# The first two softmaxes ahead of the weight decode in a fused attention and MLP kernel: a reordered prologue on one core

## The chip, the core and the metric

The kernel runs on one core of one Trainium2 chip. The metric is device time in microseconds (us) of one execution, lower is better. Everything below is fp32 data; the big matmuls run as three fp32r products of a high and a low part.

## What is computed

Cut to what matters, the reference is

```python
# attention: q, k, v are (4, 8, 576, 64); factor = 4
q_d, k_d, v_d = means over groups of 4 positions            # 144 pooled positions
out_up  = repeat(softmax(q_d k_d^T / 8) v_d, 4)              # pooled attention
mask    = abs(i - j) < 4                                     # local attention
out_loc = softmax(where(mask, q k^T / 8, -1e9)) v
x = (out_up + out_loc) as (4, 576, 512)
# both softmaxes divide by (sum + 1e-9)
# MLP 1
xn = (x - mean) / sqrt(var + 1e-6) * g_ln
x  = x + relu(xn @ w_ch1) @ w_ch2                            # 512 -> 2048 -> 512
# MLP 2 (time mix with the previous position)
k = relu(xk @ w_k); v = (k * k) @ w_v; r = sigmoid(xr @ w_r)
out = r * v
```

The weights arrive as 64-bit floats and are turned into fp32 on the chip ("decoded").

## The kernel before

**Chunks and units.** The attention works on 8 chunks `c` (half a sequence, 288 positions) times 4 head pairs `hp`. One `unit(c, hp)` is the attention of a chunk for one head pair: DVE sums queries (`qd`, L251) and, in even chunks, keys (`kdz`, L255) over groups of 4; PE computes local scores (L272) and pooled scores (L276) into the PSUM tile `sc`; DVE takes the row maximum of the pooled scores (`mx<-sc`, L279), ACT the exponential (`Pd`, L283); DVE masks the local scores into `P` (L280), subtracts their maximum, ACT the exponential (L289); DVE sums (L297), adds 1e-9 (L298), inverts, scales and transposes (`T`, L304); ACT copies the transposed tile to `PT` (four copies, L308); PE transposes `Pd` (L319), multiplies by the values into `av` (L328, L335); ACT copies `ud` (L342) and DVE adds both into `x` (L343). `sc` has one buffer, so the next unit's scores wait for the exponential. `kz` (keys) holds the two heads of a pair on the two halves of the partitions, with zeros in the other half; `kdz` is laid out alike.

**MLP 1.** For every chunk, 16 feature blocks `f` go through PE: L1 (`h_ps`, 12 matmuls), a relu and split on ACT and DVE (`hh` L500, `hl` L501), L2 (`acc`, 12 matmuls). The steps of the next chunk's attention are fed in between (`slot`).

**Weight decode.** w_ch1 and w_ch2 are cut into 32 pieces of 128x512. A piece is one DMA of 512 KB (`raw`, L123), then ACT L75, DVE L76, ACT L79, DVE L80 (the fp32 value), then its split: ACT `split_hi` (L83) and DVE `split_lo` (L86). So ACT and DVE take turns, two rounds for the decode and one for the split. `conv_gen` does one piece in two steps.

**What sets the order.** The prologue is the loop before the main loop: the four units of chunk 0 and its normalisation are fed step by step, and from the 24th round on (PRO0) every second round (PRO1) takes one step of the decode. The scheduler that builds the program may move instructions of an engine against each other; those given to `in_order` keep their program order. Each engine then runs its own list strictly in that order. All loads stand in the one queue of SP; the string ORDER says in which order the first ones do (a, b: queries and keys of units 0 and 1; c: values; m: mask and vectors; w: a pair of weight pieces). After the prologue PE starts with L1 of chunk 0; the rest of the 32 pieces are decoded while PE works on chunk 0.

**MLP 2** follows after the last chunk; no line of it is changed.

Of the kernel before, what the change touches and what calls it, by code (L numbers as in the profile page):

```python
# [19 lines left out]
B, H, S, D = 4, 8, 576, 64  # L20
DM, DF, DK = 512, 2048, 1024
SD = S // 4
N = S // 2
NCH = 2 * B
NHP = H // 2
QD = SD // 2
WIN = 30
# [9 lines left out]
def tile_block(ctx: ExitStack, tc: tile.TileContext, qT, kT, vw, vr, vec, mask, w1, w2, wk, wv, wr, out):  # L37
    nc = tc.nc
# [19 lines left out]
    pin = actx.enter_context(tc.tile_pool(name="pin", bufs=2))  # L58
# [11 lines left out]
    def decode(raw, pinned=False):  # L70

        top = raw.bitcast(U8).rearrange("p (n t) -> p n t", t=8)[:, :, 3]
        rm = stg.tile([128, 2, 512], U32, tag="stg", name="rm", bufs=RB)
        ru, m = rm[:, 0], rm[:, 1]
        in_order(pinned, nc.scalar.activation(ru.bitcast(F32), raw.rearrange("p (n t) -> p n t", t=2)[:, :, 1].bitcast(F32), AF.Copy, scale=2.0 ** -112))  # L75
        in_order(pinned, nc.vector.tensor_scalar(m, ru, 0x80000000, None, op0=ALU.bitwise_and))  # L76
        yield
        low = m.bitcast(U8).rearrange("p (n t) -> p n t", t=4)[:, :, 0]
        nc.scalar.activation(low, top, AF.Copy, scale=1.0 / 32.0, bias=-31.0 / 64.0)  # L79
        nc.vector.scalar_tensor_tensor(raw[:, 0:512].bitcast(U32), ru, 3, m, op0=ALU.logical_shift_left, op1=ALU.bitwise_or)  # L80

    def split_hi(hi, w):
        nc.scalar.copy(hi, w)  # L83

    def split_lo(hi, lo, w):
        nc.vector.tensor_tensor(lo, w, hi.bitcast(F32), op=ALU.subtract)  # L86

    def wtiles(nm):
        return [wpool.tile([128, 4, 512], F32R, tag="w", name=f"{nm}{t}") for t in "hl"]
# [12 lines left out]
    def conv_gen():  # L102
        keys = list(pieces_w12())
        raws, todo = {}, iter(keys)

        def fetch():
            key = next(todo, None)
            while key in raws:
                key = next(todo, None)
            if key is None:  # L110
                return
            nm, p, k = key
            src = w1s[:, :, 1024 * p:1024 * p + 1024] if nm == "w1" else w2s[:, 4 * p:4 * p + 4, :]
            if nm == "w2" and p == 3:
                t = xp.tile([128, 1024], I32, tag=("ah", "al")[k % 2], name="raw", bufs=ABUF)
                nc.sync.dma_start(t, src[:, k])
                raws[key] = t
            else:
                t = wpool.tile([128, 2, 1024], I32, tag="w", name="raw")
                for i in range(2):  # L120
                    raws[nm, p, k + i] = t[:, i]
                for i in range(2):
                    nc.sync.dma_start(t[:, i], src[:, k + i])  # L123

        for _ in range(ORDER.count("w")):
            fetch()
            yield
        for _ in range(AHEAD - ORDER.count("w")):
            fetch()
        last = None  # L130
        for n, key in enumerate(keys + [None]):
            if last:
                split_hi(h, w)
            if key:
                nm, p, k = key
                W = W1 if nm == "w1" else W2
                if p not in W:
                    W[p] = wtiles(f"{nm}_{p}")
                raw = raws[key]
                g = decode(raw)  # L140
                next(g)
            yield
            if key:
                next(g, None)
            if last:
                split_lo(h, l, w)
                done.add(last)
            if key:
                h, l, w = W[p][0][:, k, :], W[p][1][:, k, :], raw[:, 0:512].bitcast(F32)
            last = key  # L150
            if n % 2 == 1 or n > 24:
                fetch()
            yield
# [69 lines left out]
    def load_v(c, hp):  # L223
        b, half = divmod(c, 2)
        v = pin.tile([128, 3, 2, D], F32, tag="v", name="v", bufs=3)
        nc.sync.dma_start(v, vw[b, hp, half])
        if half == 0:
            vd = pkd.tile([QD, 2, 128], F32, tag=f"vd{hp}", name="vd")
            vdt[hp] = vd
            for t in range(2):  # L230
                r = pin.tile([QD, 4, 128], F32, tag="vr", name="r", bufs=VB)
                nc.sync.dma_start(r, vr[b, hp, :, t])
                nc.gpsimd.tensor_tensor(r[:, 0:2, :], r[:, 0:2, :], r[:, 2:4, :], op=ALU.add)
                nc.gpsimd.tensor_tensor(vd[:, t, :], r[:, 0, :], r[:, 1, :], op=ALU.add)
        vts[c, hp] = v

    def unit(c, hp, nxt):
        half = c % 2
        if nxt is not None and nxt not in loaded:
            load_qk(*nxt)  # L240
        if nxt is not None and nxt not in vts:
            load_v(*nxt)
        q, k = loaded.pop((c, hp))
        v = vts.pop((c, hp))
        if hp == 0:
# [1 line left out]
        x = xt[c]  # L247
        i = hp % 2
        P, PT = Ps[i], PTs[i]
        qd = pat.tile([128, QD], F32, tag="qd", name="qd")  # L250
        nc.vector.tensor_reduce(qd, q[:, 0:N].rearrange("p (t r) -> p t r", r=4), axis=AX.X, op=ALU.add)  # L251
        if half == 0:
            for h in range(2):
                p = slice(64 * h, 64 * h + 64)
                nc.vector.tensor_reduce(kdz[hp][p, h, :], k[p, h, 3:3 + S].rearrange("p (t r) -> p t r", r=4), axis=AX.X, op=ALU.add)  # L255
        kd, vd = kdz[hp], vdt[hp]
        yield 1600 if half == 0 else 360
        if half == 0:
# [20 lines left out]
        nc.vector.tensor_reduce(m, scd, axis=AX.X, op=ALU.max)  # L279
        nc.vector.tensor_tensor(Pl.rearrange("p (h n) w -> p h n w", h=2), scl, mask_t[:, half].unsqueeze(1).to_broadcast([128, 2, 3, WIN]), op=ALU.min)  # L280
        nc.vector.tensor_scalar(m, m, -0.125 / 16.0, None, op0=ALU.mult)  # L281
        for h in range(2):
            nc.scalar.activation(Pd[:, h, :], scd[:, h, :], AF.Exp, bias=m[:, h:h + 1], scale=0.125 / 16.0, accum_out=sm[0:QD, 6 + h:7 + h])  # L283
        yield 800
# [9 lines left out]
        for h in range(2):  # L294
            nc.scalar.activation(Pd[:, h, :], Pd[:, h, :], AF.Copy, scale=mx[0:QD, 6 + h:7 + h])
        yield 400
        nc.vector.tensor_reduce(sm[:, 0:6], Pl, axis=AX.X, op=ALU.add)  # L297
        nc.vector.tensor_scalar(sm[:, 0:6], sm[:, 0:6], 1e-9, None, op0=ALU.add)  # L298
        nc.vector.reciprocal(mx[:, 0:6], sm[:, 0:6])
        yield 600  # L300
        nc.vector.tensor_tensor(Pl, Pl, mx[:, 0:6].unsqueeze(2).to_broadcast([128, 6, WIN]), op=ALU.mult)
# [264 lines left out]
    nc.scalar.copy(ones_r, ones)  # L566
    for i in range(2):
        nc.gpsimd.memset(Ps[i], 0.0)
        nc.gpsimd.memset(PTs[i], 0.0)
    for hp in range(NHP):  # L570
        nc.gpsimd.memset(kdz[hp][0:64, 1, :], 0.0)
        nc.gpsimd.memset(kdz[hp][64:128, 0, :], 0.0)
    nc.vector.tensor_scalar(omu, vec_t[:, 1:3, :], -1.0, 1.0, op0=ALU.mult, op1=ALU.add)

    first = Attn(None, 0)
    i = 0
    while not first.over():
        first.feed(PROB)
        i += 1
        if i >= PRO0 and i % PRO1 == 0:  # L580
            next(conv, None)

    def ensure(*key):
# [166 lines left out]
RB = 3  # L750
HB = 2
AHEAD = 3
PRE = 5
LB0 = 12
RATE = 900
RATEO = 1200
RATE0 = 700
PROB = 800
PRO0 = 24
PRO1 = 2  # L760
GAP = -1
ORDER = "awmbcw"
VB = 1


def _layout(inputs):
    import numpy as np

    q, k, v = (np.asarray(inputs[n]) for n in "qkv")
    f = q.dtype  # L770

    def pairsT(a, left, right):
        t = a.transpose(0, 1, 3, 2).reshape(B, NHP, 128, S)
        return np.ascontiguousarray(np.pad(t, ((0, 0), (0, 0), (0, 0), (left, right))))

    vp = np.pad(v, ((0, 0), (0, 0), (3, 5), (0, 0)))
    idx = (24 * np.arange(24)[:, None] + np.arange(32)[None, :]).reshape(2, 3, 4, 32)
    vwin = vp[:, :, idx, :].reshape(B, NHP, 2, 2, 3, 4, 32, D)
    vwin = vwin.transpose(0, 1, 3, 5, 6, 4, 2, 7).reshape(B, NHP, 2, 128, 3, 2, D)
    vr = v.reshape(B, NHP, 2, 2, QD, 4, D).transpose(0, 1, 4, 3, 5, 2, 6).reshape(B, NHP, QD, 2, 4, 128)  # L780
    vec = np.stack([np.asarray(inputs[n]).reshape(KT, 128).T for n in ("moe_g_ln", "moe2_mu_k", "moe2_mu_r")], axis=1)

    r = np.arange(32)[:, None]
    w = np.arange(WIN)[None, :]
    mask = np.empty((4, 32, 2, 3, WIN), f)
    for half in range(2):
        for n in range(3):
            for j in range(4):
                i0 = N * half + 96 * n + 24 * j
                key = i0 - 3 + w  # L790
                ok = (np.abs(i0 + r - key) < 4) & (key >= 0) & (key < S)
                mask[j, :, half, n, :] = np.where(ok, 3.0e38, -8.0e9)
    c = np.ascontiguousarray
    return {
        "qT": pairsT(q, 0, 8), "kT": pairsT(k, 3, 3), "vw": c(vwin), "vr": c(vr), "vec": c(vec),
        "mask": c(mask.reshape(128, 2, 3, WIN)),
        **{n: c(inputs[m]).view(np.int64) for n, m in WEIGHTS},
    }
# [17 lines left out]
```

## Time and profile before

| | |
|---|---|
| median of 3 runs | 803.0 us (802.44 to 803.74) |
| the profiled execution | 801.98 us, its span 799.9 us |
| busy in the span | PE 758.2 us (95%), DVE 546.4 (68%), ACT 398.7 (50%), POOL 76.6 (10%) |
| granted TensorE clock, mean | 0.998 of full speed |
| before PE's first L1 matmul (0 to 53.4 us) | PE 19.15 us busy, DVE 42.83, ACT 37.04 |

The span is the time from the first to the last instruction that the profile has. "Busy" counts an instruction from its start to its end; PE's busy share says little of how full PE is, since matmuls overlap. A line number is that of the kernel before; the changed kernel's lines are some 8 to 9 higher from `unit` on.

### The profile page before, as it was taken

The page shows a single profiled execution, that of the slowest core. Times are in us where ns is not written, and L with a number is a line of the kernel's source. Part 1 is how long each engine was busy: PE and PEld are TensorE (multiplying, and loading weights), DVE is VectorE, ACT ScalarE, POOL GpSimd, SP SyncE. Part 2 cuts the span into 40 slices and gives each one's busy share as a digit, 9 for nine tenths or more (in the row PEclk, how much of TensorE's full clock was granted, in tenths as well). Part 3 has the DMA queues.
Part 4 walks back from the last instruction along what each step waited for, and adds up shares of the span by engine and source line. Part 5 has one row for each costly group of instructions (what it writes and reads, how often), then busy time and mean ns, then how long its engine had stood idle before and what let it go on. Part 6 is the DMA issues. An engine that isn't in the chain of part 4 may idle for free.

```text
span 799.9 us, 15611 instructions
## 1 busy us (share of the span) xinstructions
PE 758.2 (95%) x6150; PEld 731.3 (91%) x6150; DVE 546.4 (68%) x1234; ACT 398.7 (50%) x995; POOL 76.6 (10%) x121
## 2 busy tenths in 40 slices
PE   2559989999999999999999999999999999999998
PEld 1349989999999999999999999999999999999998
DVE  6989997655665746665755645846959586867664
ACT  4889975543553543544553543734444353525140
POOL 3210332001131001121001001001000000000000
PEclk9999999999999999999999999999999999999999
DMA  7796533332342331451333310522020202010101
GB/s 223 231 319 230 175 100 107 114 101 79 111 142 92 105 103 58 120 163 59 109 89 109 86 50 30 186 79 70 11 69 6 74 1 80 1 40 1 41 1 40
DMA packets 43209, 76.06 MB, mean 95 GB/s; under 512 B 4608, under 2 KB 28288, under 8 KB 43136
## 3 DMA queue, kind: packets, MB, share of 16 engines
q1 hardware_dynamic: 43136, 75.07, 29.8%
q8 instruction: 48, 0.79, 0.4%
q14 instruction: 25, 0.20, 0.1%
HBM read 60.38 MB, written 14.68 MB: 94 GB/s over the span
## 4 chain that ended last, share of the span: by engine, by line
PE 83%; DVE 7%; DMA 5%; ACT 4%; issue 1%; SPq 0%; ACTq 0%
PE b_ps L196 10%; PE b_ps L195 10%; PE b_ps L197 10%; PE h_ps L195 8%; PE acc L195 7%; PE acc L196 7%; PE acc L197 7%; PE h_ps L196 7%; PE h_ps L197 7%; DMA raw<-in_w 4%; PE av L328 2%; PE sc L276 2%; PE sc L272 2%; DVE raw L80 1%; PE tp L319 1%; PE av L335 1%
## 5 line engine op out<-in xcount | busy, mean ns | idle before, releaser
L501 DVE SCALAR_TENSOR_TENSOR hl<-h_ps,hh 128x288 fp32r<-128x288 f32 x128 | 57.8, 453 | 85.5 <-ACT hh L500 85.0
L500 ACT ACTIVATE hh<-h_ps 128x288 fp32r<-128x288 f32 x128 | 51.6, 405 | 80.1 <-PE h_ps L197 79.3
L197 PE MATMUL b_ps<-xk,wbl 128*128 128x384 f32 x192 | 64.9, 338 | 0.0
L195 PE MATMUL b_ps<-xk,wbh 128*128 128x384 f32 x192 | 64.9, 338 | 0.0
L196 PE MATMUL b_ps<-xk,wbh 128*128 128x384 f32 x192 | 64.8, 338 | 0.0
L197 PE MATMUL b_ps<-k,wbl 128*128 128x384 f32 x192 | 64.1, 334 | 0.0
L195 PE MATMUL b_ps<-k,wbh 128*128 128x384 f32 x192 | 64.1, 334 | 0.0
L196 PE MATMUL b_ps<-k,wbh 128*128 128x384 f32 x192 | 64.1, 334 | 0.0
L728 DVE RECIPROCAL e<-e 128x384 f32<-128x384 f32 x24 | 61.1, 2544 | 0.1
L308 ACT COPY PT<-T 32x144 f32<-32x144 f32 x128 | 39.6, 309 | 32.5 <-DVE T L304 31.1
L521 POOL TENSOR_TENSOR x<-x2t,x 128x288 f32<-128x288 f32 x32 | 25.4, 826 | 294.7 <-DVE x2t L520 236.4
L708 ACT ACTIVATE kr<-b_ps 128x384 f32<-128x384 f32 x48 | 23.5, 490 | 46.9 <-PE b_ps L197 46.9
L647 ACT ACTIVATE mixa<-x2in,vec_t 128x384 f32<-128x384 f32 x48 | 28.1, 613 | 37.3 <-DVE xr L650 34.8
L80 DVE SCALAR_TENSOR_TENSOR raw<-rm 128x512 uint32<-128x512 uint32 x52 | 37.2, 720 | 12.0 <-ACT rm L79 11.7
L709 DVE TENSOR_TENSOR kr<-kr,b_ps 128x384 f32<-128x384 f32 x48 | 26.5, 552 | 25.8 <-ACT kr L708 25.8
L79 ACT ACTIVATE rm<-raw 128x512 uint8<-128x512 uint8 x52 | 39.9, 784 | 7.0 <-DVE rm L76 6.7
L283 ACT ACTIVATE Pd<-sc,mx 72x144 f32<-72x144 f32 x64 | 23.4, 370 | 37.6 <-DVE mx L281 37.5
L195 PE MATMUL acc<-hh,w_1h 128*128 128x288 f32 x128 | 40.4, 319 | 1.0 <-ACT hh L500 1.0
L195 PE MATMUL h_ps<-ah,w_0h 128*128 128x288 f32 x128 | 39.4, 309 | 1.2 <-ACT ah L394 1.2
L698 DVE TENSOR_TENSOR k<-kr,k 128x384 fp32r<-128x384 f32 x48 | 26.7, 556 | 19.8 <-ACT k L697 19.7
L195 PE MATMUL h_ps<-ah,w_2h 128*128 128x288 f32 x128 | 40.0, 312 | 0.0
L195 PE MATMUL acc<-hh,w_2h 128*128 128x288 f32 x128 | 39.9, 315 | 0.0
(160 smaller groups left out, 2560.4 us busy)
## 6 DMA issues: line engine op xcount, KB each, us to landing
raw<-in_w SPq DMA_DIRECT2D x32, 512.0 KB
v<-in_vw SPq DMA_DIRECT2D x32, 192.0 KB
bd<-raw SPq DMA_DIRECT2D x20, 256.0 KB
wf<-bd SPq DMA_DIRECT2D x10, 512.0 KB
q<-in_qT SPq DMA_DIRECT2D x32, 148.0 KB
kz<-in_kT SPq DMA_DIRECT2D x32, 145.5 KB
r<-in_vr SPq DMA_DIRECT2D x32, 144.0 KB
x2d<-x SPq DMA_DIRECT2D x8, 576.0 KB
```

Of the source, the lines that this page charges most:

```text
L79: nc.scalar.activation(low, top, AF.Copy, scale=1.0 / 32.0, bias=-31.0 / 64.0)
L80: nc.vector.scalar_tensor_tensor(raw[:, 0:512].bitcast(U32), ru, 3, m, op0=ALU.logical_shift_left, op1=ALU.bitwise_or)
L195: nc.tensor.matmul(ps, wh, ah, start=first, stop=False)
L196: nc.tensor.matmul(ps, wh, al, start=False, stop=False)
L197: nc.tensor.matmul(ps, wl, ah, start=False, stop=last)
L308: nc.scalar.copy(PT[p, :, j, :], T[p, :, 0:24])
L500: nc.scalar.activation(hh, ps[:, 0:N], AF.Relu)
L501: nc.vector.scalar_tensor_tensor(hl, ps[:, 0:N], 0.0, hh.bitcast(F32), op0=ALU.max, op1=ALU.subtract)
L647: nc.scalar.activation(a2, t[:, k, :, 1:SEG + 1], AF.Copy, scale=vec_t[:, 1 + which, k:k + 1])
L698: nc.vector.tensor_tensor(l, r, h.bitcast(F32), op=ALU.subtract)
L709: nc.vector.tensor_tensor(r, r, ps[:, 0:NB], op=ALU.mult)
L728: nc.vector.reciprocal(e, e)
```

## The change

Four things. The unit's sums are cut out into `prep`, which makes one instruction of the two key sums (over 128 partitions and both heads; the zeros of `kz` give the zeros of `kdz`, whose clearing on POOL goes); in chunk 0 the next unit's `prep` is called inside the unit, right behind its maximum, and keeps its program order. All steps of the first PINNED = 6 pieces keep their program order. The addition of 1e-9 to the local sums (L298) goes: column 30 of `P` is set to 1e-9 once, and the sum takes 31 columns; the host clears the two spare rows of the value windows. ORDER puts the first weight pair behind the mask and the second unit's queries and keys, and the decode takes two of every five rounds, from the 5th on.

```diff
-        nc.scalar.activation(low, top, AF.Copy, scale=1.0 / 32.0, bias=-31.0 / 64.0)
-        nc.vector.scalar_tensor_tensor(raw[:, 0:512].bitcast(U32), ru, 3, m, ...)
+        in_order(pinned, nc.scalar.activation(low, top, AF.Copy, scale=1.0 / 32.0, bias=-31.0 / 64.0))
+        in_order(pinned, nc.vector.scalar_tensor_tensor(raw[:, 0:512].bitcast(U32), ru, 3, m, ...))
...
         for n, key in enumerate(keys + [None]):
+            pin = n < PINNED
             if last:
-                split_hi(h, w)
+                in_order(pin, split_hi(h, w))
...
-                g = decode(raw)
+                g = decode(raw, pin)
...
-                split_lo(h, l, w)
+                in_order(pin, split_lo(h, l, w))
...
+    def prep(c, hp):
+        q, k = loaded[c, hp]
+        qd = pat.tile([128, QD], F32, tag="qd", name="qd")
+        qds[c, hp] = qd
+        in_order(c == 0, nc.vector.tensor_reduce(qd, q[:, 0:N].rearrange("p (t r) -> p t r", r=4), axis=AX.X, op=ALU.add))
+        if c % 2 == 0:
+            in_order(c == 0, nc.vector.tensor_reduce(kdz[hp], k[:, :, 3:3 + S].rearrange("p h (t r) -> p h t r", r=4), axis=AX.X, op=ALU.add))
...
+        if (c, hp) not in qds:
+            prep(c, hp)
...
-        qd = pat.tile([128, QD], F32, tag="qd", name="qd")
-        nc.vector.tensor_reduce(qd, q[:, 0:N]...)
-        if half == 0:
-            for h in range(2):
-                p = slice(64 * h, 64 * h + 64)
-                nc.vector.tensor_reduce(kdz[hp][p, h, :], k[p, h, 3:3 + S]...)
+        qd = qds.pop((c, hp))
...
         nc.vector.tensor_scalar(m, m, -0.125 / 16.0, None, op0=ALU.mult)
+        if c == 0 and nxt in loaded:
+            prep(*nxt)
...
-        nc.vector.tensor_reduce(sm[:, 0:6], Pl, axis=AX.X, op=ALU.add)
-        nc.vector.tensor_scalar(sm[:, 0:6], sm[:, 0:6], 1e-9, None, op0=ALU.add)
+        nc.vector.tensor_reduce(sm[:, 0:6], P[:, :, 0:WIN + 1], axis=AX.X, op=ALU.add)
...
+        nc.gpsimd.memset(Ps[i][:, :, WIN:WIN + 1], 1e-9)
-    for hp in range(NHP):
-        nc.gpsimd.memset(kdz[hp][0:64, 1, :], 0.0)
-        nc.gpsimd.memset(kdz[hp][64:128, 0, :], 0.0)
...
-        if i >= PRO0 and i % PRO1 == 0:
+        if i >= PRO0 and i % 5 in (0, 2):
             next(conv, None)
...
+PINNED = 6
-PRO0 = 24
-PRO1 = 2
+PRO0 = 5
-ORDER = "awmbcw"
+ORDER = "ambwcw"
...
+    vwin[..., WIN:, :] = 0
```

How the built programs differ, at the three places that the prediction speaks of. `kz_106` and `kz_107` are the two key buffers, `P_112`/`PT_104` those of the first (and third) unit, `P_113`/`PT_105` those of the second (and fourth).

SP's queue from its start, before:

```order
L215 DMA q<-in_qT 128x296
L220 DMA kz_106<-in_kT 64x582 x2
L123 DMA raw<-in_w 128x1024 x2
L556 DMA mask_t<-in_mask 128x180
L557 DMA vec_t<-in_vec 128x12
L215 DMA q<-in_qT 128x296
L220 DMA kz_107<-in_kT 64x582 x2
L226 DMA v<-in_vw 128x384
```

and in the changed kernel:

```order
L217 DMA q<-in_qT 128x296
L222 DMA kz_106<-in_kT 64x582 x2
L565 DMA mask_t<-in_mask 128x180
L566 DMA vec_t<-in_vec 128x12
L217 DMA q<-in_qT 128x296
L222 DMA kz_107<-in_kT 64x582 x2
L123 DMA raw<-in_w 128x1024 x2
L228 DMA v<-in_vw 128x384
```

The first weight pair moved behind five other loads. (On ACT the first decode step, L75 of the first piece, stands ahead of the first unit's exponential in both programs.)

ACT from the first unit's `PT` copies and the second unit's exponential to the first unit's `ud`, before:

```order
L308 COPY PT_104<-T 32x6x24 x4
L283 ACTIVATE Pd,sm<-sc,mx 72x144 x2
L289 ACTIVATE P_113<-P_113 128x6x30
L79 ACTIVATE rm<-raw 128x512
L342 COPY ud<-av 128x72
```

and in the changed kernel:

```order
L293 ACTIVATE Pd,sm<-sc,mx 72x144 x2
L299 ACTIVATE P_113<-P_113 128x6x30
L317 COPY PT_104<-T 32x6x24 x3
L83 CAST w_0h<-raw 128x512
L75 ACTIVATE rm<-raw 128x512
L317 COPY PT_104<-T 32x6x24
L305 ACTIVATE Pd<-Pd,mx 72x144 x2
L79 ACTIVATE rm<-raw 128x512
L317 COPY PT_105<-T 32x6x24 x4
L83 CAST w_0h<-raw 128x512
L75 ACTIVATE rm<-raw 128x512
L351 COPY ud<-av 128x72
```

Ahead of `ud` there are now two L83, two L75, the scaling of the second unit's `Pd` (two) and its four `PT` copies.

DVE from the first unit's `x` to the third unit's pooled maximum, before:

```order
L343 TENSOR_TENSOR x<-av,ud 128x288
L255 TENSOR_REDUCE kdz_110<-kz_106 64x144 x2
L298 TENSOR_SCALAR sm<-sm 128x6
L76 TENSOR_SCALAR rm<-rm 128x512
L299 RECIPROCAL mx<-sm 128x6
L301 TENSOR_TENSOR P_113<-P_113,mx 128x6x30
L279 TENSOR_REDUCE mx<-sc 72x2
```

and in the changed kernel:

```order
L352 TENSOR_TENSOR x<-av,ud 128x288
L80 SCALAR_TENSOR_TENSOR raw<-rm 128x512
L86 TENSOR_TENSOR w_0l<-raw,w_0h 128x512
L244 TENSOR_REDUCE qd<-q 128x72
L76 TENSOR_SCALAR rm<-rm 128x512
L246 TENSOR_REDUCE kdz_110<-kz_106 128x288
L80 SCALAR_TENSOR_TENSOR raw<-rm 128x512
L86 TENSOR_TENSOR w_0l<-raw,w_0h 128x512
L287 TENSOR_REDUCE mx<-sc 72x2
```

The rest of the second unit's softmax moved ahead of `x`; in its place stand the third unit's query sum and the ends of two weight pieces.

## Rows read from the trace of the kernel before

**Rows 1.** Windows: us of stretch, busy us of PE, PEld, DVE, ACT, POOL (instructions), clock, DMA.

```profile
0.00:14.30 14.30, 2.03 (x26) 0.94 (x26) 7.11 (x13) 4.45 (x6) 6.14 (x23) 1.00 0.77 226
14.30:53.40 39.10, 17.12 (x176) 11.61 (x176) 35.72 (x94) 32.59 (x85) 10.20 (x14) 1.00 0.78 248
...
80.00:100.00 20.00, 20.00 (x216) 18.75 (x216) 19.76 (x54) 19.64 (x50) 6.36 (x8) 1.00 0.58 175
...
200.00:300.00 100.00, 100.00 (x989) 95.26 (x989) 60.79 (x174) 49.23 (x146) 13.15 (x20) 1.00 0.35 111
```

**Rows 2.** Waits of PE from 53 to 160 us: total, times, longest.

```profile
PE tp L319 <- ACT Pd L295: 2.4, 1, 2.4
...
PE h_ps L196 <- DVE al L397: 0.6, 1, 0.6
```

**Rows 3.** Timeline of PE: start, duration, instruction, idle before.

```profile
53.42 0.85 PE L195 MATMUL h_ps<-ah,w_0h 128*128 128x288 f32 x2 [1.21 <-ACT ah L394]
```

**Rows 4.** Timeline of SP's queue, the issues of loads.

```profile
1.18 1.19 SPq L220 DMA_DIRECT2D kz<-in_kT  x2
2.41 1.06 SPq L123 DMA_DIRECT2D raw<-in_w  x2
3.51 0.43 SPq L556 DMA_DIRECT2D mask_t<-in_mask  x1
...
6.96 0.58 SPq L226 DMA_DIRECT2D v<-in_vw  x1
...
14.95 0.36 SPq L215 DMA_DIRECT2D q<-in_qT  x1
```

**Rows 5.** Timeline of ACT in the prologue.

```profile
7.86 0.66 ACT L75 ACTIVATE rm<-raw 128x512 f32<-128x512 f32 x1 [5.25 <-DMA raw<-in_w]
...
15.34 0.38 ACT L283 ACTIVATE Pd<-sc,mx 72x144 f32<-72x144 f32 x1 [3.19 <-DVE mx L281]
...
19.08 1.27 ACT L308 COPY PT<-T 32x144 f32<-32x144 f32 x4
...
22.27 0.72 ACT L295 ACTIVATE Pd<-Pd,mx 72x144 f32<-72x144 f32 x2
```

**Rows 6.** Timeline of DVE in the prologue.

```profile
4.29 1.53 DVE L255 TENSOR_REDUCE kdz<-kz 64x144 f32<-64x576 f32 x2 [0.84 <-DMA kz<-in_kT]
...
14.33 0.45 DVE L279 TENSOR_REDUCE mx<-sc 72x2 f32<-72x288 f32 x1
...
18.25 0.45 DVE L279 TENSOR_REDUCE mx<-sc 72x2 f32<-72x288 f32 x1
...
22.86 0.45 DVE L343 TENSOR_TENSOR x<-av,ud 128x288 f32<-128x288 f32 x1
...
26.08 0.45 DVE L279 TENSOR_REDUCE mx<-sc 72x2 f32<-72x288 f32 x1
...
34.60 0.41 DVE L279 TENSOR_REDUCE mx<-sc 72x2 f32<-72x288 f32 x1
```

**Rows 7.** Groups by line, 0 to 53.4 us: busy us, mean ns, idle before.

```profile
L75 ACT ACTIVATE rm<-raw 128x512 f32<-128x512 f32 x13 | 8.5, 659 | 5.7 <-DMA raw<-in_w 5.7
L80 DVE SCALAR_TENSOR_TENSOR raw<-rm 128x512 uint32<-128x512 uint32 x10 | 7.5, 747 | 2.3 <-ACT rm L79 2.3
...
L255 DVE TENSOR_REDUCE kdz<-kz 64x144 f32<-64x576 f32 x8 | 5.9, 744 | 1.0 <-DMA kz<-in_kT 0.8
L86 DVE TENSOR_TENSOR w_0l<-raw,w_0h 128x512 fp32r<-128x512 f32 x7 | 5.3, 753 | 0.2 <-ACT w_0h L83 0.2
...
L76 DVE TENSOR_SCALAR rm<-rm 128x512 uint32<-128x512 uint32 x12 | 4.9, 415 | 3.1 <-ACT rm L75 3.1
...
L83 ACT CAST w_0h<-raw 128x512 fp32r<-128x512 f32 x7 | 4.3, 615 | 0.0
...
L251 DVE TENSOR_REDUCE qd<-q 128x72 f32<-128x288 f32 x5 | 2.2, 435 | 0.8 <-DMA q<-in_qT 0.8
...
L298 DVE TENSOR_SCALAR sm<-sm 128x6 f32<-128x6 f32 x4 | 1.6, 406 | 0.1
```

More of the change, by code (lines that the diff above doesn't have):

```diff
@@ L78, in decode @@
         low = m.bitcast(U8).rearrange("p (n t) -> p n t", t=4)[:, :, 0]
-        nc.scalar.activation(low, top, AF.Copy, scale=1.0 / 32.0, bias=-31.0 / 64.0)
-        nc.vector.scalar_tensor_tensor(raw[:, 0:512].bitcast(U32), ru, 3, m, op0=ALU.logical_shift_left, op1=ALU.bitwise_or)
+        in_order(pinned, nc.scalar.activation(low, top, AF.Copy, scale=1.0 / 32.0, bias=-31.0 / 64.0))
+        in_order(pinned, nc.vector.scalar_tensor_tensor(raw[:, 0:512].bitcast(U32), ru, 3, m, op0=ALU.logical_shift_left, op1=ALU.bitwise_or))
     def split_hi(hi, w):
-        nc.scalar.copy(hi, w)
+        return nc.scalar.copy(hi, w)
     def split_lo(hi, lo, w):
-        nc.vector.tensor_tensor(lo, w, hi.bitcast(F32), op=ALU.subtract)
+        return nc.vector.tensor_tensor(lo, w, hi.bitcast(F32), op=ALU.subtract)
     def wtiles(nm):
@@ L200, in tile_block @@
     loaded = {}
+    qds = {}
     vdt = {}
@@ L249, in unit @@
         P, PT = Ps[i], PTs[i]
-        qd = pat.tile([128, QD], F32, tag="qd", name="qd")
-        nc.vector.tensor_reduce(qd, q[:, 0:N].rearrange("p (t r) -> p t r", r=4), axis=AX.X, op=ALU.add)
-        if half == 0:
-            for h in range(2):
-                p = slice(64 * h, 64 * h + 64)
-                nc.vector.tensor_reduce(kdz[hp][p, h, :], k[p, h, 3:3 + S].rearrange("p (t r) -> p t r", r=4), axis=AX.X, op=ALU.add)
+        qd = qds.pop((c, hp))
         kd, vd = kdz[hp], vdt[hp]
```

## The prediction, made before the changed kernel ran

> **What bounds the kernel now.** I read the table of windows first, then PE's waits, then the prologue on SP, ACT and DVE by their timelines. From the first L1 matmul at 53.42 us [rows 3] PE works without a break: in the stretch 200 to 300 it is busy all the time while DVE has 61 and ACT 49 of 100 us [rows 1]. So an instruction saved on DVE or POOL in chunks 1 to 7 is worth nothing, and only two things can move the end: when the first L1 matmul starts, and what PE waits for in chunk 0. In the prologue PE is idle most of the time; DVE is busy 35.7 of the 39.1 us from 14.3 on [rows 1], with two sorts of work that share it: four attention units and ten weight pieces. In chunk 0 DVE and ACT are full too (19.76 and 19.64 of 20 us between 80 and 100) [rows 1], and PE waits there twice, 2.4 us for the scaled `Pd` and 0.6 us for `al` [rows 2].
>
> **The sum** is made against the profiled execution (801.98 us, 1.0 under the median of 803.0); the change that it gives is added to the median.
>
> *Small edits.* L298 goes 32 times, 4 of them in the prologue (1.6 us of DVE there [rows 7]). One key sum over 1152 columns replaces two over 576 at 744 ns each [rows 7]: between 744 ns (if the halves ran at once) and 1.49 us; since both heads' columns now pass through every partition I take 1.35, two of the old less one start. The sum over 31 instead of 30 columns, the clearing of column 30 (POOL) and the clearings that go (POOL, before anything waits) I cost at nothing: POOL is busy 6 of the first 14 us [rows 1]. Were POOL's cover gone, it would be some tenths, once. In chunks 1 to 7 all this lies beside a full PE.
>
> *First exponential.* It used to come at 15.34 [rows 5], because the second unit's sums and two pieces stood ahead of the first maximum at 14.33 [rows 6]. Now the sums of unit 1 lead to a maximum at about 8.5, but on ACT the first L75 still stands ahead of the exponential, and it waits for a weight load that now stands behind five others. Those took SP from 3.51 to 6.96 [rows 4], 3.45 us, so the load is issued at 5.9, or at 5.0 if the second q load takes the 0.36 us that the third took [rows 4] in place of its 1.2; I take 5.45. Issue to L75's start was 7.86 - 2.41 = 5.45 us [rows 4, 5]; that gives 10.9. With L75 (0.66) the exponential comes at 11.6: **3.7 us earlier**. The second unit's maximum then falls on 18.25 - 3.7 = 14.55 [rows 6].
>
> *Second maximum to first `x`.* This took 22.86 - 18.25 = 4.6 us [rows 6]. ACT's list now has, ahead of `ud`, two L83 (615 ns), two L75 (659 ns) [rows 7], four `PT` copies (1.27) and two scalings of `Pd` (0.72) [rows 5] that it did not have there: 4.5 us, and ACT runs its list in order, so `ud` and DVE's `x` wait for them. `x` falls on 14.55 + 4.6 + 4.5 = 23.7. **The lead is gone**: 0.8 us later than before.
>
> *First `x` to third maximum.* Before, 26.08 - 22.86 = 3.2 us [rows 6]. Now DVE has between them `x` (0.45 [rows 6]), two L80 (747), two L86 (753), `qd` (435), L76 (415 ns) [rows 7] and the key sum (1.35): 5.65 us, less 0.5 for starts that overlap the end before by some 0.07 each, plus the turns with ACT: idle ahead of L80 and L76 is 2.3/10 and 3.1/12 us in the mean [rows 7], 0.7 for these three. Makes 5.9, so the third maximum falls on 29.6, **3.5 us late**. The third unit's scores wait for the key sum, and PE, ACT and the `PT` copies for them.
>
> *Third to fourth maximum.* Before 8.5 us [rows 6], with four decode instructions of DVE in it; the new order has eight: three more L76, one more L80, 2.0 us by their means [rows 7], 1.0 for their turns with ACT, less L298 (0.4) and 0.5 of overlapping starts. So 2.1 more: **5.6 late**, at 40.2 in place of 34.60.
>
> *Fourth maximum to L1.* Before 53.42 - 34.60 = 18.8 us [rows 3, 6] with 21 decode instructions of DVE; now 16: two L76, one L80, two L86 fewer, 3.1 us by their means less 0.3 of overlap. So 16.0: the first L1 matmul at 56.2, **2.8 us late**. In all the order up to the normalisation's first row holds eleven ends of pieces (L86) where it held ten, so the prologue does one piece more, not less.
>
> *Chunk 0.* PE's list there is unchanged, but it starts later beside the same full DVE and ACT. Followed with the same means, the new order removes the 2.4 us wait for `Pd`, keeps the 0.6, and brings three: 0.8 before the first unit of chunk 1 multiplies by its values, 0.6 at the last low halves of w_3, 2.5 at an `acc` that takes a late `hl`. 4.5 against 3.0: **+1.5**, an estimate; its bounds are -2.4 (the wait for `Pd` goes, nothing comes) and +4.
>
> Sum: +2.8 + 1.5 = +4.3 us, 806.3 for a profiled execution and **807.3 us** for the median.
>
> **A page against this sum.** The term that everything hangs on is the 5.45 us from issue to landing. The other row for it is that of the keys: issued at 1.18, their sum starts at 4.29 [rows 4, 6], 3.1 us for 146 KB. The Trainium skill, "DMA: Bandwidth & Descriptors", section "Anatomy of one DMA", fits a DMA as 2.0 us and the bytes at 436 GB/s, which makes an estimate of 3.2 us for the 512 KB of a piece; the row of the piece disagrees, that of the keys (2.3 by the fit) is nearer. What a short landing would do is the second rival.
>
> **Rivals.**
> 1. *The lead survives (faster).* If ACT and DVE kept up, DVE's work alone would set the start: 7.11 + 35.72 [rows 1], plus one piece (415 + 747 + 753 ns), less 1.6 for L298 and 0.5 for the key sums [rows 7], is 42.6 us; with the old idle of 7.2 in the head less 3.7, and 3.4 after it, L1 starts at 49.5: 3.9 us early, 799.1. It decides at the first `x`: at or before 20 us, and the third maximum at or before 23. For it: DVE is the fullest engine, and less is asked of it early. Against it: the pinned order on ACT ahead of `ud`. Chance 0.07.
> 2. *Weights land quickly.* The 5.45 us were the first loads of the program, and the keys needed only 3.1. By that the piece is there 2.35 us sooner and the whole chain with it: 805.0. That is what the page's fit makes of it. Against it: three q and k loads now stand directly ahead of the piece in the queue. Chance 0.17.
> 3. *Chunk 0 absorbs it (no change).* DVE and ACT pace chunk 0; one piece less (1.9 us of DVE) is left for it, so of 2.8 only 0.9 arrive, and with the wait for `Pd` gone -1.5: about 803. For it: both are full there. Against it: PE has no slack to catch up with, its matmuls stand back to back. Chance 0.12.
> 4. *Worse.* The load is issued at 5.9 and chunk 0's new waits come at their upper end: 2.8 + 0.4 + 4 = 7.2, 810.2. Chance 0.11.
>
> That the change doesn't do what it says is part of this: the first two maxima do move ahead of the decode, but the decode then stands ahead of units 3 and 4.
>
> **How the numbers follow.** Forecast 0.53; rivals 0.07, 0.17, 0.12, 0.11. Faster by over 0.2% (1.6 us, about what a measurement of this kernel can tell from no change) is rival 1: 0.07. Within it is rival 3: 0.12. Slower is the rest: 0.81. The range goes from 803.2, which takes in the upper half of rival 3, to 810.6, the end of rival 4; it leaves out rival 1, half of rival 3 and a tail above, some 0.18.
>
> **What would show it.** Right step by step: ACT's first L75 at 10 to 11.5 with a wait for the load ahead of it; second maximum near 14.5; first `x` near 23.7 with ACT busy ahead of `ud`; maxima of units 3 and 4 near 29.6 and 40; first L1 near 56; chunks 1 to 7 as before; PE's waits in chunk 0 some 4 us in place of 3. Wrong: a first L75 before 9; a first `x` before 22, or a third maximum before 27; a first L1 before 54; or a time lost or won after chunk 0, where I have none.

## The result, and the profile after

The changed kernel takes **808.69 us** (median of 4 runs, 807.14 to 809.11) against 802.72 us (median of 4, 801.97 to 803.74): ratio 1.0074, 95% interval 1.0059 to 1.0089, slower. The forecast was 807.3 in a range of 803.2 to 810.6. The profiled execution took 808.65 us, its span 806.9 against 799.9. One execution among all the runs of this document, one of the kernel without pins, took 1253.89 us at a mean granted clock of 0.577, a slower state, and is left out of every number here.

All but 0.2 us of the 7.0 is lost before chunk 1. PE's first L1 matmul:

```profile
59.24 0.61 PE L196 MATMUL h_ps<-ah,w_0h 128*128 128x288 f32 x1 [1.24 <-ACT ah L403]
```

It starts 5.8 us late [rows 3]. As the end of chunk 0 I take the start of the 385th matmul record of the MLP (a few records are missing, so this is good to some 0.3 us): 131.07 against 124.29, 6.8 us late. The next chunk takes 61.4 us in both.

**Where the time is.** The windows up to chunk 1, of the changed kernel (columns as in [rows 1]):

```profile
0.00:14.30 14.30, 4.54 (x56) 2.47 (x56) 7.09 (x17) 4.55 (x12) 4.04 (x16) 1.00 0.76 235
14.30:59.20 44.90, 15.26 (x146) 9.87 (x146) 35.13 (x85) 34.53 (x83) 10.33 (x16) 1.00 0.70 219
59.20:131.10 71.90, 68.78 (x595) 64.29 (x596) 65.32 (x155) 58.83 (x139) 14.78 (x17) 0.98 0.55 180
0.00:131.10 131.10, 88.58 (x797) 76.62 (x798) 107.54 (x255) 97.92 (x232) 29.14 (x48) 0.99 0.62 199
```

and of the kernel before, where [rows 1] has the first two:

```profile
53.40:124.30 70.90, 67.78 (x595) 63.75 (x596) 66.52 (x161) 60.69 (x141) 15.35 (x17) 0.98 0.57 186
0.00:124.30 124.30, 86.93 (x797) 76.30 (x798) 109.35 (x266) 97.72 (x231) 31.70 (x54) 0.99 0.66 210
```

Read the third figure, DVE. Up to chunk 1 it has 1.8 us *less* work (107.54 for 109.35), and is idle 23.6 us in place of 14.9. Of the 8.6 us more, none is in the first 14.3 us (7.2 in both), 6.4 lie between there and the first L1 matmul (44.90 - 35.13 = 9.8 against 39.10 - 35.72 = 3.4), and 2.2 in chunk 0. The change saved work on the fullest engine and paid with its idle time. What DVE waits for between 14.3 us and L1, after:

```profile
DVE raw L80 <- ACT rm L79: 3.2, 5, 1.4
DVE mx L287 <- PE sc L284: 3.2, 1, 3.2
DVE rm L76 <- ACT rm L75: 2.0, 2, 1.0
DVE w_1l L86 <- ACT w_1h L83: 0.5, 1, 0.5
```

and before:

```profile
DVE sm L292 <- ACT Pd L283: 1.3, 2, 1.0
DVE raw L80 <- ACT rm L79: 1.1, 2, 0.8
DVE w_0l L86 <- ACT w_0h L83: 0.2, 1, 0.2
```

Two new idle times: one wait of 3.2 us for the third unit's pooled scores, and 4.1 us more for ACT's steps of the decode (L80 2.1, L76 2.0).

**The one wait of 3.2 us.** All engines around it, after (the timeline, as in [rows 3]):

```profile
24.76 0.72 POOL L235 TENSOR_TENSOR r<-r 72x256 f32<-72x256 f32 x1 [5.61 <-DMA r<-in_vr]
...
26.37 0.33 SPq L234 DMA_DIRECT2D r<-in_vr  x1
...
26.84 0.83 PE L280 MATMUL sc<-kz,q 128*32 128x60 f32 x24
...
28.51 0.68 DVE L86 TENSOR_TENSOR w_0l<-raw,w_0h 128x512 fp32r<-128x512 f32 x1
...
30.18 0.45 POOL L236 TENSOR_TENSOR vd<-r 72x128 f32<-72x128 f32 x1
...
30.68 0.50 PE L344 MATMUL av<-PdT,vd 72*64 72x72 f32 x2 [3.02 <-POOL vd L236]
...
31.11 1.24 PE L284 MATMUL sc<-kdz,qd 128*72 128x288 f32 x2
...
32.38 0.45 DVE L287 TENSOR_REDUCE mx<-sc 72x2 f32<-72x288 f32 x1 [3.19 <-PE sc L284]
```

DVE is through with its decode work at 28.51 + 0.68 = 29.2. The third unit's pooled scores (L284) stand in PE's list behind the second unit's product with the pooled values (L344), which waits 3.0 us until POOL has made `vd`. In the kernel before PE's list had the scores (L276) ahead of those products (L335), and the values were there early:

```profile
18.07 0.33 SPq L232 DMA_DIRECT2D r<-in_vr  x1
...
20.80 0.72 POOL L233 TENSOR_TENSOR r<-r 72x256 f32<-72x256 f32 x1 [2.75 <-DMA r<-in_vr]
...
21.60 0.46 POOL L234 TENSOR_TENSOR vd<-r 72x128 f32<-72x128 f32 x1
...
24.81 1.23 PE L276 MATMUL sc<-kdz,qd 128*72 128x288 f32 x2
...
25.36 0.59 POOL L234 TENSOR_TENSOR vd<-r 72x128 f32<-72x128 f32 x1
...
29.24 0.45 PE L335 MATMUL av<-PdT,vd 72*64 72x72 f32 x4
```

(A wait of PE for `vd` is not new in itself: the kernel before has one of 2.99 us at 47.46, for the fourth unit. New is its place, ahead of the third unit's scores.) Why `vd` is late stands in SP's queue of the changed kernel:

```profile
16.07 0.89 SPq L123 DMA_DIRECT2D raw<-in_w  x2
19.18 0.33 SPq L234 DMA_DIRECT2D r<-in_vr  x1
19.60 0.34 SPq L217 DMA_DIRECT2D q<-in_qT  x1
20.03 1.11 SPq L222 DMA_DIRECT2D kz<-in_kT  x2
26.37 0.33 SPq L234 DMA_DIRECT2D r<-in_vr  x1
...
31.09 0.34 SPq L217 DMA_DIRECT2D q<-in_qT  x1
```

The raw values `r` have one buffer: each load waits in SP's queue until POOL has pooled the one before, and everything behind it waits too. The early decode put a weight pair (two loads of 512 KB) at 16.07 into this chain. The `r` issued at 19.18 is used by POOL at 24.76, 5.6 us later; before, the one issued at 18.07 was used at 20.80, 2.7 us later. The kernel before shows the same delay where a pair goes ahead of a value load later on: pair at 22.90, the `r` behind it issued at 25.98 and used at 30.89, 4.9 us later. In the changed kernel the loads behind that chain are late from then on: the fourth unit's queries are issued at 31.09, where they went at 18.90.

**Chunk 0.** PE's waits from 54 to 160 us, after, to set against [rows 2]:

```profile
PE acc L197 <- DVE hl L510: 2.5, 1, 2.5
PE mean L377 <- DVE xsum L364: 1.8, 1, 1.8
PE h_ps L196 <- ACT ah L403: 1.2, 1, 1.2
PE av L337 <- ACT PdT L331: 0.3, 1, 0.3
```

The second and third still belong to the prologue. The wait for `Pd` is gone, that of an `acc` for `hl` came. A shorter one shows only in PE's weight loads (PEld), for the low halves of w_3:

```profile
PEld h_ps L198 <- DVE w_3l L86: 0.8, 4, 0.3
```

### The profile page after: what moved, and what is told of

It is laid out like the page before. It is cut to its first block, busy times and chain, and to the rows that moved or that the text cites. A ratio compares the mean times of both kernels' runs of the same rounds, so it can differ in the third digit from the quotient of the medians.

```text
span 806.9 us, 15566 instructions
## 1 busy us (share of the span) xinstructions
PE 759.8 (94%) x6150; PEld 731.5 (91%) x6150; DVE 538.2 (67%) x1186; ACT 398.2 (49%) x995; POOL 73.6 (9%) x115
## 4 chain that ended last, share of the span: by engine, by line
PE 83%; DMA 5%; ACT 5%; DVE 3%; SPq 1%; issue 1%; POOL 1%; ACTq 0%; POOLq 0%; DVEq 0%
PE b_ps L197 10%; PE b_ps L196 10%; PE b_ps L198 10%; PE h_ps L196 8%; PE h_ps L197 7%; PE acc L196 7%; PE h_ps L198 7%; PE acc L197 7%; PE acc L198 7%; DMA r<-in_vr 3%; PE av L337 2%; PE sc L284 2%; DMA raw<-in_w 2%; PE sc L280 1%; ACT rm L79 1%; ACT rm L75 1%
## 5 line engine op out<-in xcount | busy, mean ns | idle before, releaser
L510 DVE SCALAR_TENSOR_TENSOR hl<-h_ps,hh 128x288 fp32r<-128x288 f32 x128 | 57.8, 453 | 90.8 <-ACT hh L509 90.1
L317 ACT COPY PT<-T 32x144 f32<-32x144 f32 x128 | 39.5, 309 | 18.9 <-DVE T L313 17.4
L715 ACT ACTIVATE kr<-b_ps 128x384 f32<-128x384 f32 x48 | 23.6, 491 | 46.9 <-PE b_ps L198 46.9
L80 DVE SCALAR_TENSOR_TENSOR raw<-rm 128x512 uint32<-128x512 uint32 x52 | 36.8, 711 | 12.1 <-ACT rm L79 11.7
L293 ACT ACTIVATE Pd<-sc,mx 72x144 f32<-72x144 f32 x64 | 23.5, 369 | 41.2 <-DVE mx L289 41.2
L79 ACT ACTIVATE rm<-raw 128x512 uint8<-128x512 uint8 x52 | 40.2, 785 | 2.6 <-DVE rm L76 2.4
L197 PE MATMUL acc<-hl,w_2h 128*128 128x288 f32 x128 | 38.1, 298 | 2.5 <-DVE hl L510 2.5
L235 POOL TENSOR_TENSOR r<-r 72x256 f32<-72x256 f32 x32 | 27.5, 859 | 136.9 <-DMA r<-in_vr 136.9
```

Source lines behind the costliest of these rows:

```text
L79: in_order(pinned, nc.scalar.activation(low, top, AF.Copy, scale=1.0 / 32.0, bias=-31.0 / 64.0))
L80: in_order(pinned, nc.vector.scalar_tensor_tensor(raw[:, 0:512].bitcast(U32), ru, 3, m, op0=ALU.logical_shift_left, op1=ALU.bitwise_or))
L197: nc.tensor.matmul(ps, wh, al, start=False, stop=False)
L317: nc.scalar.copy(PT[p, :, j, :], T[p, :, 0:24])
L510: nc.vector.scalar_tensor_tensor(hl, ps[:, 0:N], 0.0, hh.bitcast(F32), op0=ALU.max, op1=ALU.subtract)
```

## The experiments

Each theory is about which part of the change carries the loss. The first four runs do one part alone or undo one; the next ones undo two or three, then work on the value loads. Intervals are for the ratio to the kernel before on the same chip.

**The small edits alone.** The loads, the pace and the free order of the kernel before, with the key sum in one instruction and the spare column:

```diff
-PINNED = 6
+PINNED = 0
-        if i >= PRO0 and i % 5 in (0, 2):
+        if i >= PRO0 and i % 2 == 0:
-        if c == 0 and nxt in loaded:
-            prep(*nxt)
-ORDER = "ambwcw"
+ORDER = "awmbcw"
```

(PRO0 is 24 again as well, and the sums are free in their order.)

> The spare column for eps, the single key sum and the sums cut out into prep, with the order of loads, the pace of the decode and the free order of its instructions as before. My theory (the loss comes from the pinned decode ahead of the units and from the values' loads behind the weight pairs): no difference, 802 to 804 us, first L1 matmul within 1 us of 53.4. Rival (the small edits cost by themselves, for instance the 1152-column key sum on DVE): 2 us or more above before, with the first L1 late.

Measured: 803.87 us, ratio 1.0019 (1.0009 to 1.0030). The first L1 matmul at 52.97. As expected they are not the loss, but they don't pay either, although DVE's work up to chunk 1 is 0.4 us less: by the interval they cost 0.7 to 2.4 us.

**The old order of the first loads**, all else as changed:

```diff
-ORDER = "ambwcw"
+ORDER = "awmbcw"
```

> The changed kernel with the loads in the old order (first weight pair ahead of mask and second unit). Theory: the pinned decode still stands ahead of the units, so still 4 to 7 us above before; first L1 near 57 to 59. Rival (the weight pair behind five loads is what costs, since ACT's first step waits for it): back to within 1.5 us of before.

Measured: 809.67, ratio 1.0089 (1.0076 to 1.0102), 7.3 us above before; first L1 matmul at 57.24, chunk 0 75.4 us long. The order of the first loads alone doesn't carry the loss.

**No pins**, all else as changed:

```diff
-PINNED = 6
+PINNED = 0
```

> The changed kernel with PINNED = 0: the first six pieces may be moved by the scheduler again. Theory: units 1 to 4 are no longer held up behind decode instructions, the fourth maximum comes some 2 us earlier and the first L1 1.5 to 3 us earlier than in the changed kernel; total 804 to 807. If the late pooled values of unit 2 stay (3 us wait of PE for vd near 28), the gain stops there. Rival (pins don't matter, the pace does): same as the changed kernel, 808 to 809.

Measured: 809.9, ratio 1.0081 (1.0065 to 1.0098), a miss of my 804 to 807 and near the rival's 808 to 809. The fourth maximum comes 1.9 us and the first L1 matmul 1.4 us earlier than in the changed kernel (41.88 and 57.83), but chunk 0 is 73.7 us long and gives it back. The third maximum stays at 32.43, and PE's waits from 20 to 60 us still have the late values:

```profile
PE av L344 <- POOL vd L236: 2.7, 1, 2.7
```

So the early pace alone, without pins, gives the late units 3 and 4.

**The old pace**, with pins and the new loads:

```diff
-        if i >= PRO0 and i % 5 in (0, 2):
+        if i >= PRO0 and i % 2 == 0:
-PRO0 = 5
+PRO0 = 24
```

> The changed kernel with the old pace (decode from the 24th round, every second), pins and load order as changed. Theory: the decode stands behind the units again, third and fourth maximum 3 to 8 us earlier than in the changed kernel (near 26 and 32), first L1 at 52.5 to 55; but the six pinned pieces now fall later and chunk 0 pays for it, by 3 us or more: total 805 to 811. Rival (the early pace alone is the loss and nothing else): at or below before, 801 to 803.

Measured: 809.5, ratio 1.0080 (1.0067 to 1.0094). The maxima of units 3 and 4 come at 25.3 and 32.22 and the first L1 matmul at 53.80: the prologue is as good as before. But chunk 0 takes 76.4 us, and PE's waits there (from 54 to 140 us) are now for weights:

```profile
PE acc L196 <- ACT w_2h L83: 2.2, 1, 2.2
PE acc L196 <- ACT w_3h L83: 1.2, 1, 1.2
```

DVE is busy only 30.13 of the 39.5 us from 14.3 on (windows), 5.6 less than before [rows 1]: it waits 5.5 us there for ACT's decode steps (L75 3.3, L79 2.2), and the work falls to chunk 0 (69.14 us of DVE there against 66.52). The waits are not all of the longer chunk: PE is idle 5.8 us of it against 3.1, and busy 2.8 us longer (70.62 against 67.78), with a granted clock of 0.94 in the mean against 0.98.

**Pace and pins undone together**, the new loads and the sums moved ahead kept: the two edits above in one.

> The changed kernel with two parts undone together: the old start and pace of the weight decode (from pass 24 of the first chunk's prologue, every second pass) and no pieces of it pinned in place. The new order of the first loads, the sums of query and key moved ahead and the small edits stay. Theory A (pins and pace are two faces of one thing, decode work put ahead of what the first chunk's units need: early pace delays units 3 and 4 by the late pooled values, late pace with pins makes chunk 0 some 5 us longer; either alone is enough for the loss): the first matmul of chunk 0 at 51.5 to 53, chunk 0 71 to 72.5 us long, chunk 1 at 122 to 125, time 801 to 805. Theory B (the loss is in what stays: the new order of the loads, with weights landing late, and the small edits): as slow as the changed kernel, 807 to 810, chunk 1 at 129 or later.

Measured: **802.43**, ratio 0.9995 (0.9978 to 1.0012): no difference from before. First L1 matmul at 52.53, chunk 0 70.6 us. The windows:

```profile
14.30:52.50 38.20, 15.14 (x148) 9.57 (x146) 33.25 (x81) 31.67 (x79) 10.98 (x15) 0.70 0.75 247
52.50:123.10 70.60, 67.58 (x600) 62.65 (x601) 65.50 (x156) 59.98 (x141) 14.41 (x17) 0.97 0.56 188
```

With the new loads kept, neither undone costs 6 us (808.69), either one undone some 7 (809.5, 809.9), both undone none (802.43). The two parts don't add: theory A holds, theory B falls.

**The old loads as well** (ORDER as in the second run, on top of the last).

> As the run before, and the old order of the first loads too: of the change only the sums moved ahead and the small edits are left. Theory A: 802 to 805, like the small edits alone (803.9), first matmul of chunk 0 at 52.5 to 54. Theory B: faster by 3 us or more than the run before, since the load order is undone. A third reading (moving the sums ahead is itself a cost, as VectorE serves unit 2 before unit 1's exponential): slower than the small edits alone by over 1.5 us, that is 805.5 or more.

Measured: 803.19, ratio 1.0003 (0.9994 to 1.0012); first L1 matmul at 53.14. Theory A again. The order of the loads and the sums moved ahead make no difference that can be told.

**A small dose of the early pace**: no pins, old pace, two passes brought forward:

```diff
-        if i >= PRO0 and i % 2 == 0:
+        if i in (5, 10) or i >= PRO0 and i % 2 == 0:
```

> The changed kernel with the pins gone and the old pace (the run of 802.43), but two passes of the weight decode brought forward to the prologue's passes 5 and 10: a small dose of the early pace. Theory A (a pass taken early puts its weight pair and its decode work ahead of what units 3 and 4 need, on the one SP queue and in VectorE's order): the third maximum of the pooled scores 28.5 to 31 instead of 25.95, the first matmul of chunk 0 at 53 to 54.5 instead of 52.53, time 803.5 to 806. Rival (there is room for early decode while VectorE idles in units 1 and 2; only the full early pace overfills it): third maximum 25 to 27, first matmul of chunk 0 at or before 52.7, chunk 0 no longer than 70.6, time 800.5 to 802.8.

Measured: 805.08, ratio 1.0023 (1.0012 to 1.0034); third maximum at 31.80 (0.8 later than theory A had it), first L1 matmul at 54.41. The rival is refuted. The two passes brought one weight pair into the chain of value loads, at 15.71, and that pair is enough to make the values late:

```profile
15.71 0.90 SPq L123 DMA_DIRECT2D raw<-in_w  x2
...
18.95 0.33 SPq L234 DMA_DIRECT2D r<-in_vr  x1
...
23.95 1.20 POOL L235 TENSOR_TENSOR r<-r 72x256 f32<-72x256 f32 x1 [5.03 <-DMA r<-in_vr]
```

In the run before this one with the new loads (802.43) no weight load stands between 8.7 and 23.5 us, and the same `r` goes at 18.59 and is used at 21.07. One pair costs 2.5 us of landing (5.0 against 2.5), and PE then waits 3.0 us for `vd` at 30.09, as in the changed kernel.

**Two buffers for the raw values**, in the changed kernel:

```diff
-VB = 1
+VB = 2
```

> The changed kernel with two buffers instead of one for the raw values that GpSimd pools, so that a load of them no longer waits for the pooling of the one before. Theory A (3 us of the 5.8 by which chunk 0 starts late are TensorE's wait for pooled values, at 30.7 in the changed kernel's trace): the wait of 3.0 us at 30.7 is gone, the third maximum of the pooled scores comes before 30.5 instead of 32.38, the first matmul of chunk 0 at 56 to 58.5 instead of 59.24, time 805 to 808. Theory B (VectorE and ScalarE are so filled with pinned decode work that the wait only hides it): the wait goes, the first matmul of chunk 0 stays within 1 us of 59.24, time 808 to 809.5. Theory C (the values are late because the DMA queues are full of weights, not because of the single buffer): the wait at about 30.7 stays at 2 us or more.

Measured: 809.45, ratio 1.0079 (1.0067 to 1.0092). None of the three as written: the wait for `vd` goes (against C), the third maximum hardly moves, 32.12 (against A), the first L1 matmul comes 1.6 us earlier at 57.67 (against B), and the time is B's. PE:

```profile
27.03 0.83 PE L280 MATMUL sc<-kz,q 128*32 128x60 f32 x24 [1.57 <-DMA kz<-in_kT]
30.31 1.24 PE L284 MATMUL sc<-kdz,qd 128*72 128x288 f32 x2 [2.44 <-DVE kdz L246]
```

and DVE:

```profile
28.91 1.35 DVE L246 TENSOR_REDUCE kdz<-kz 128x288 f32<-128x1152 f32 x1
30.17 1.17 DVE L80 SCALAR_TENSOR_TENSOR raw<-rm 128x512 uint32<-128x512 uint32 x1
31.26 0.94 DVE L86 TENSOR_TENSOR w_0l<-raw,w_0h 128x512 fp32r<-128x512 f32 x1
32.12 0.44 DVE L287 TENSOR_REDUCE mx<-sc 72x2 f32<-72x288 f32 x1
```

With the values in time, the keys are late (the next in the same queue behind weights), then the key sum and the pinned pieces ahead of the maximum. Three latenesses lie one under the other; taking away the top one shows the next.

**The same in the kernel before** (VB = 2, nothing else).

> The kernel before with two buffers for the raw values, nothing else: the control of the run before, and a version that could be faster than both. If the single buffer costs the kernel before too, the first matmul of chunk 0 comes at 48 to 51.5 instead of 53.42 and the time is 800 to 802.5 if chunk 0 keeps its 70.9 us; if chunk 0 then meets its weights late, chunk 0 is 73 to 79 us long and the time is 803 to 808. If the single buffer costs the kernel before nothing, within 1 us of the kernel before.

Measured: 805.93, ratio 1.0037 (1.0023 to 1.0051). The first L1 matmul does come 3.8 us earlier, at 49.63, and chunk 0 takes 80.0 us:

```profile
14.30:49.60 35.30, 17.05 (x176) 11.11 (x176) 30.06 (x82) 26.93 (x75) 9.24 (x16) 1.00 0.92 321
49.60:129.60 80.00, 73.11 (x620) 66.35 (x621) 71.50 (x170) 65.51 (x151) 12.76 (x18) 0.96 0.47 153
```

DVE did 5.7 us less between 14.3 us and L1 than before [rows 1] and 5.0 more in chunk 0 (71.50 against 66.52). An earlier L1 with less decoded is no gain. PE's waits in chunk 0 are not for weights, as I had expected (0.2 us): they are for the attention of chunk 1, 2.7 us for `Pd` and 2.1 for `PdT`. Why chunk 0 is as much as 9.1 us longer is not shown in full.

**The values through GpSimd's own queue**, in the changed kernel:

```diff
-                nc.sync.dma_start(r, vr[b, hp, :, t])
+                nc.gpsimd.dma_start(r, vr[b, hp, :, t])
```

> The changed kernel with the raw values loaded by GpSimd's own DMA queue instead of SP's, so that SP no longer stands still behind a load that waits for the pooling before it. Theory A1 (SP's standing still makes the queries and keys of units 3 and 4 late): those of unit 4 are issued before 26 instead of 31.09, the third maximum comes before 30 instead of 32.38, the first matmul of chunk 0 at 55 to 57.5 instead of 59.24; time 805 to 808.5, the less if chunk 0 then waits for weights. Theory A2 (what is late is late because weights take the transfer's time, in whatever queue; as with two buffers): the third maximum stays at 31.5 or later, the first matmul of chunk 0 at 57.5 or later, time 808 to 810.

Measured: 814.68, ratio 1.0144 (1.0129 to 1.0160), a miss for both: the third maximum comes at 27.76, as A1 had it, the first L1 matmul at 61.71, later than either. SP no longer stands still and issues 24 weight pieces by 60 us where the changed kernel issued 19, and the values land later: 6.6 us in the median, against 2.5 to 5.6 from issue to use in the changed kernel (behind the first). DMA issues from 0 to 60 us (KB each, median us to landing):

```profile
raw<-in_w SPq DMA_DIRECT2D x24, 512.0 KB, 7.8
...
r<-in_vr POOLq DMA_DIRECT2D x9, 144.0 KB, 6.6
```

PE waits for `vd` 3.4 us at 33.64 and 4.0 us at 47.24.

**The same on the version of 802.43.**

> The same edit on the kernel with pace and pins undone (802.43): a version that could be faster than both. TensorE waited 3.9 us there for the pooled values of unit 4, at 47.5. If the single chain of value loads through SP costs it time: the first matmul of chunk 0 at 48.5 to 51 instead of 52.53 and, with chunk 0 at its 70.6 us, 799 to 801. If chunk 0's end is set by the weight decode, as the kernel before with two value buffers suggests (its chunk 0 began 3.8 us earlier and took 9.1 us longer): chunk 0 is longer by as much or more, time 802 to 807.

Measured: 812.72, ratio 1.0119 (1.0105 to 1.0133), a miss too: first L1 matmul at 59.97. PE's waits up to 140 us:

```profile
PE av L344 <- POOL vd L236: 10.8, 4, 6.5
```

In both of these a separate queue gave the small loads nothing; the weights beside them had no stop any more. The Trainium skill, "DMA: Bandwidth & Descriptors", section "Issuing engines are not separate DMA queues", has the rule: all issuing engines share the same 16 DMA engines. The landing times (6.6 us against 2.5 to 5.6) agree with it; that it is the whole cause was not shown here, since the issue by GpSimd itself changed too.

**All runs together.** DVE's busy and idle time up to chunk 1, from the windows of each run's profiled execution (us); the last column is the median of its runs (the two kernels' own from the result; the experiments ran on three chips, where the kernel before has 802.41, 802.87 and 803.18). Work plus idle is the start of chunk 1 by definition; what the table adds is that the work hardly differs:

| run | first L1 | DVE work | DVE idle | chunk 1 | median |
|---|---|---|---|---|---|
| pace and pins undone | 52.5 | 106.0 | 17.1 | 123.1 | 802.43 |
| kernel before | 53.4 | 109.4 | 14.9 | 124.3 | 802.72 |
| pace, pins and loads undone | 53.1 | 105.0 | 19.6 | 124.6 | 803.19 |
| small edits alone | 53.0 | 108.9 | 16.2 | 125.1 | 803.87 |
| two early passes | 54.4 | 107.0 | 20.6 | 127.6 | 805.08 |
| before, two value buffers | 49.6 | 109.7 | 19.9 | 129.6 | 805.93 |
| old pace | 53.8 | 107.1 | 23.1 | 130.2 | 809.50 |
| **changed kernel** | 59.2 | 107.5 | 23.6 | 131.1 | 808.69 |
| no pins | 57.8 | 106.9 | 24.6 | 131.5 | 809.90 |
| two value buffers | 57.7 | 108.4 | 23.2 | 131.6 | 809.45 |
| old loads | 57.2 | 108.5 | 24.2 | 132.7 | 809.67 |
| values' own queue, pace and pins undone | 60.0 | 106.2 | 28.2 | 134.4 | 812.72 |
| values' own queue | 61.7 | 110.3 | 24.5 | 134.8 | 814.68 |

The work spans 5.3 us without following the time; the idle spans 13 and follows it in the large, though not row by row (19.6 at 803.19, 19.9 at 805.93). The first L1 matmul alone does not (49.6 and 53.8 in slow kernels).

## Why the prediction was right, and where a step failed

The time was held by the range, and the sign and mechanism (the softmaxes move ahead, the decode then stands ahead of units 3 and 4) were as forecast. That it was held with a term missing is in part luck: on the profiled executions the sum said +4.3 us and +6.7 came (808.65 against 801.98), and the range reached that far up for rival 4, whose chain did not occur. By its steps:

- *First exponential.* Predicted load issue 5.45, first L75 10.9, exponential 11.6. Measured 5.14, 10.27 and 10.84:

```profile
10.27 0.66 ACT L75 ACTIVATE rm<-raw 128x512 f32<-128x512 f32 x1 [7.65 <-DMA raw<-in_w]
10.84 0.36 ACT L293 ACTIVATE Pd<-sc,mx 72x144 f32<-72x144 f32 x1
```

  The landing took 10.27 - 5.14 = 5.13 us, near the 5.45 of [rows 4, 5]. Rival 2, weights that land quickly, is refuted. The prediction's estimate of 3.2 us for this load, from the fit in the Trainium skill, "DMA: Bandwidth & Descriptors", section "Anatomy of one DMA", falls with it; that section makes its fit for DMAs on GpSimd's path, and this load is issued by SP, so the miss says nothing of the fit itself.
- *Second maximum to first `x`.* Predicted 14.55 and 23.7; measured 13.73 and 23.27. Right: 9.5 us for 9.1, ACT's list ahead of `ud` eats the lead. Rival 1 fell here, at the place it named.
- *First `x` to third maximum.* Predicted 29.6, measured 32.38. **This step failed.** The text had it that the third unit's scores wait for the key sum. DVE's part of the sum was right (its list reached the maximum at 29.2), but PE's was missing; the wait of PE for `vd` stood at nothing. PE's list has the second unit's product with `vd` ahead of those scores, and `vd` came 3.0 us too late, because a weight pair had gone into the queue ahead of the third value load. I had read SP's queue at its start only, not where it meets the pace of the decode, and PE's order at this place not at all.
- *Third to fourth maximum.* Predicted 10.6, measured 43.80 - 32.38 = 11.4; *fourth to L1* predicted 16.0, measured 15.4. Right within 0.8, and the errors cancel. So L1 came 3.0 us later than forecast (59.24 for 56.2): the failed step brought 3.2 (32.38 - 23.27 = 9.1 for 5.9), the others -0.2 together.
- *Chunk 0.* Predicted +1.5, measured 131.07 - 59.24 = 71.8 against 70.9, +0.9. Of the waits, that for `Pd` goes and the 2.5 us for `hl` come, as forecast; the 0.6 us at w_3's low halves are 0.8, in PE's weight loads. The 0.8 ahead of the first unit's values did not come (0.3, for `PdT`, at the third unit), and the 0.6 for `al`, which was to stay, went. In all 3.6 us of waits for the 3.0 before, where 4.5 were forecast; the other 0.3 of the +0.9 is within what the end of chunk 0 is good to. Rival 3 (chunk 0 absorbs it) fell: it absorbed nothing. (Its figures, +0.9 and -1.5, make 801.5 to 803.9 rather than "about 803".) Rival 4's chain (a load issued at 5.9, chunk 0's waits at their upper end) did not occur either.
- *Small edits.* Predicted about nothing. Alone they were 1.5 us slower (0.7 to 2.4 by the interval), where nothing had been forecast; with all other parts undone but the sums ahead, 0.3, within the interval of no change. Why the two differ is open. The key sum over 1152 columns took 1.33 us in the mean, 1.35 assumed.

The other new idle time of DVE, 4.1 us for ACT's decode steps, is no error of the sum: it lies in the steps that came out within 0.8 us. Nor is it the pins' alone: without them DVE's idle time from 14.3 us to L1 is 43.5 - 33.4 = 10.1 us, with 4.7 for pooled scores and 3.4 for ACT's L75 and L83.

**What stays open.** How the 7 us of each half divide exactly: each single undo also makes a new order on every engine, so the runs show that either part is enough, not a price per part. Whether the third unit's scores, put ahead of that product in PE's list, would have kept the third maximum in time although `vd` is late: no run changes PE's order alone. And whether a prologue with earlier decode can be faster at all: neither the changed kernel nor one of the eleven others beat the one before; the best (802.43) equals it.

## What to carry to other kernels

When a list of background work is started earlier, look at every queue that it shares with the foreground, above all at one that stands still for a single buffer: here one pair of weight loads between two small loads made another engine wait 3 us, and the two early passes that brought it moved the first L1 matmul by 1.9 us. Count the idle time of the fullest engine up to the point where another takes over the pace, not only its work: here the work fell by 1.8 us and the idle rose by 8.6. And two parts that each do harm may look harmless when undone one at a time; undo them together before dropping a theory.

## What the chip showed that I had not expected

- In the version of 802.43 the profiled execution had a granted clock of 0.50 (the 1.2 GHz level) from 32.4 to 52.5 us, where PE was busy 6.24 of 20.1 us, and 0.92 in the mean over the 18.1 us before, where it was busy 8.90; yet that execution took 800.82 us, the shortest of that kernel's runs, and the first L1 matmul came at 52.53. While PE waited most of the time, the lower clock cost nothing that can be seen there. (The longest of the twelve, 808.0 us, has the lowest mean clock, 0.976, so this need not hold for each.)
- An L86 that ran beside POOL's L235 and L236 took 1.22 us (at 24.81, changed kernel) where the next one took 0.68: 0.5 us that the sum, with its means, had no term for.
